# A written-out order of an attention and gated-MLP kernel replaced by another order, with paired tail stores and a last batch stored by half tiles

## The chip, the cores and the metric

The kernel runs on one core of one Trainium2 chip. The metric is the device time of one execution in microseconds (us). The core has five instruction streams that run side by side: TensorE (PE: matmuls, with PEld for its weight loads), VectorE (DVE), ScalarE (ACT), GpSimd (POOL) and SyncE (SP, which only issues transfers). Transfers between memory and the chip run on 16 DMA engines. Each stream executes its instructions strictly in the order in which they were written, so an instruction that waits holds up everything behind it on its engine.

## The reference

Eight batches, twelve heads, 448 positions, head size 64. Queries and keys are normalised by their root mean square, then softmax attention is computed, and the result of all heads (768 columns) goes through a gated MLP with a mixing over positions.

```python
def _attn_ref(q, k, v, g_q, g_k):
    q_n, k_n = (rmsnorm(q, g_q), rmsnorm(k, g_k))
    scores = scale * np.matmul(q_n, k_n.transpose(0, 1, 3, 2))
    attn = np.exp(scores - np.max(scores, axis=-1, keepdims=True))
    attn = attn / (np.sum(attn, axis=-1, keepdims=True) + 1e-09)
    return np.matmul(attn, v)

def _moe_ref(x, w_in, w_spatial, b_spatial, w_out):
    h = np.maximum(x @ w_in, 0.0)
    u, v = h[..., :d_ff // 2], h[..., d_ff // 2:]
    v_n = (v - mean(v)) / np.sqrt(var(v) + 1e-06)
    v_s = np.einsum('ts,bsd->btd', w_spatial, v_n) + b_spatial[None, :, None]
    return (u * v_s) @ w_out
```

The output is 8 x 448 x 768 in float32, 11 MB; the inputs q, k and v are 33 MB.

## The kernel before

The whole order of work is written out in one string, `PLAN`, of some 2,000 words. A loop at the end of the kernel reads it word by word and calls one function for each. A word has the form name.arguments/slots/engine: `S.5.3/01` is `op_S(G=5, u=3)` with the PSUM banks 0 and 1. No scheduler moves anything afterwards; the order of the words is the order of each engine's instructions.

Heads are taken in groups of four, so a batch b has three groups G = 3b, 3b+1 and 3b+2, and there are 24 groups. The stages of a group are these, with the letters of the words:

- `L.G.i` loads q (i = 0), k (1) or v (2) of a group as a 448 KB tile into one of ten `raw` slots (line 281; `l` are half loads of group 0). The loads are issued by SP. A slot is taken again when its last reader is done.
- `Q` squares a tile (ACT, DVE or POOL, line 373 or 375), `R` sums the squares on DVE (line 386), `I` and `J` make the inverse root on ACT (lines 399 and 404), `N` multiplies (POOL or DVE, line 419).
- `P` with `K` turn a tile by TensorE and copy it out (lines 438, 356, 457); for later groups `T` with `Z` turn it by a transposing DMA (line 474) instead.
- `S` makes scores (line 499, eight small matmuls for each word), `E` is their exponential on ACT (line 507). There are 168 of each, seven for each group.
- `F` casts v to bf16. `s`, `a` and `b` are passes over the exponentials (line 534) for the sums of the softmax and the two halves of the output; `D` and `d` invert the sums on ACT (lines 553 and 557), `X` multiplies on DVE (line 563).
- `V`, `W` and `U` are the matmuls with `w_in` (lines 579, 594, 632), `c` and `u` their relu, `B`, `M`, `m` and `A` the normalisation, `H` the mixing over positions (line 647), `G` the gate on DVE (line 654).
- `O.b.m.h` is the product with `w_out` for tile m of batch b and column half h (line 663, four matmuls), `o` copies it to one of five `os` slots (line 354 on ACT, 356 on DVE), and `t.b.m` stores the tile (lines 679 and 681). Positions 384 to 447 of two neighbouring batches share one tile, m = 3: 64 rows of each batch.
- `z.n` are n matmuls on constants in the head (line 247), `w`, `ws`, `wo` and `wb` are the loads of the weights by POOL's queue (lines 310, 325, 328 and 333), `x` copies rows of `w_in` into another order.

A copy into an `os` slot waits until the store that read the slot before has landed. That wait, the slots of `raw` and the eight PSUM banks are the couplings on which the change bears.

Of the kernel before, what the change touches and what calls it, by code (L numbers as in the profile page):

```python
# [27 lines left out]
K.1.1/1/v P.2.0/6 K.2.0/1/v P.1.0/2 K.1.0/2/v s.0.2.0/3 E.0.0/4 S.0.3/45 E.0.3/5 S.0.2/67 E.0.2/6 F.0//g a.0.6.0/0
N.2.1/3 Q.3.0/1/v s.0.6.0 s.0.3.0 a.0.3.0 a.0.2.0 S.1.4/12 E.1.4/7 Q.4.0/0/v F.1//v s.0.0.0 S.1.6/45 E.1.6/8 S.1.0/67
a.0.1.0 E.1.0/9 S.1.5/12 E.1.5/a S.1.2/45 E.1.2/b R.3.0 P.2.1/6 s.0.4.0 S.1.1/12 E.1.1/c b.0.1.0/7 b.0.4.0 L.7.0/3  # L30
a.0.0.0 s.0.5.0 S.1.3/45 E.1.3/d a.0.4.0 R.4.0 K.2.1/2/v wo w.0 a.0.5.0 s.0.1.0 S.2.6/12 b.0.3.0 s.1.0.0/6 E.2.6/e
Q.3.1/2 R.3.1 I.3 J.3 Q.4.1/1 R.4.1 a.1.3.0/4 b.0.5.0 a.1.1.0 s.1.2.0 I.4 S.2.1/12 E.2.1/f Q.5.0/0 a.1.6.0 s.1.1.0
L.2.2/8 L.5.1/5 L.6.1/0 Y.4/5 s.1.6.0 N.3.1/0/v N.3.0/1/v S.2.0/12 s.1.4.0 s.1.3.0 b.0.6.0 s.1.5.0 L.3.2/9 J.4 N.4.0/2
N.4.1/3 D.0/0 b.1.5.0/3 b.1.6.0 E.2.0/g y.4//v L.7.1/6 a.1.2.0 d.0 S.2.3/12 D.1/1 R.5.0 P.3.1/5 P.3.0/6 K.3.1/3/v
K.3.0/3/v E.2.3/h Y.1/1 y.1//v Y.0/2 y.0//v S.3.4/56 d.1 Q.6.0/2/a a.1.0.0 E.3.4/i a.1.4.0 b.1.0.0 S.3.6/12 E.3.6/j
b.0.2.0 S.3.1/56 E.3.1/k X.0.0 P.4.1/0 Q.5.1/1/v K.4.1/0/v b.1.1.0 S.2.2/12 b.1.4.0 b.1.3.0 E.2.2/l R.5.1 L.4.2/7
S.3.3/56 E.3.3/0 b.0.0.0 b.1.2.0 a.1.5.0 w.1 I.5 X.1.1 X.1.0 Y.2/0 X.0.1 y.2//v S.2.5/12 E.2.5/6 P.4.0/3 K.4.0/0/v
S.3.5/56 E.3.5/2 Y.3/4 y.3//v L.8.0/4 S.3.2/12 Q.6.1/0 R.6.1 F.2//g J.5 R.6.0 E.3.2/8 s.2.1.1/70 s.2.6.1 s.2.3.1
s.2.5.1 F.3//g S.3.0/56 a.2.1.1/34 a.2.6.1 S.2.4/12 L.5.2/8 s.2.2.1 a.2.3.1 E.3.0/9 E.2.4/1 a.2.2.1 s.2.0.1 Q.7.1/1
R.7.1 Q.7.0/0/a R.7.0 N.5.0/0 a.2.5.1 a.2.0.1 S.4.4/56 E.4.4/3 s.2.4.1 b.2.2.1/12 N.5.1/1 a.2.4.1 b.2.3.1 b.2.1.1  # L40
D.2/1 b.2.0.1 b.2.4.1 b.2.5.1 Q.8.0/2 P.5.0/5 K.5.0/2/v L.8.1/9 L.9.1/2 P.5.1/6 K.5.1/1/v I.6 D.3/0 J.6 N.6.1/3 x.2
L.9.0/5 d.2 X.2.0 V.0.2.1/7 I.7 T.6.1/0 V.0.1.1/0 N.6.0/2 T.6.0/3 d.3 b.2.6.1 S.4.1/56 V.0.1.0 V.0.2.0 X.2.1 E.4.1/c
V.0.1.2 Q.9.1/1/a X.3.1 S.5.1/56 E.5.1/7 X.3.0 S.4.0/12 E.4.0/d V.0.2.2 c.0.2//v c.0.1//v R.9.1 V.0.0.1/3 J.7 L.10.0/0
U.0.0.1/4 S.4.6/56 E.4.6/4 S.5.3/12 x.0 U.0.2.2/7 L.11.1/1 B.0.2 Q.8.1/0 U.0.0.2 V.0.0.0 F.5//g E.5.3/5 N.7.0/0/v
Z.6/3/v S.5.2/56 S.5.0/01 E.5.0/b R.8.1 N.7.1/1 T.7.1/1 U.0.0.0 U.0.1.1/2 U.0.1.2 R.8.0 u.0.0//v E.5.2/a S.4.5/01
E.4.5/8 U.0.1.0 S.6.4/56 E.6.4/l U.0.2.1 S.4.3/01 I.8 E.4.3/0 V.0.0.2 u.0.1//v c.0.0//v S.4.2/56 F.4//g Q.9.0/1
E.4.2/h J.8 N.8.1/3 U.0.3.0/4 U.0.3.2 S.5.5/01 E.5.5/f S.5.6/23 E.5.6/k B.0.1 R.9.0 U.0.2.0 U.0.3.1 s.4.0.1/56
# [673 lines left out]
```

## Time and profile before

| | us |
|---|---|
| median of three runs | 274.83 (273.71 to 276.78) |
| profiled execution, device time | 274.1 |
| its span, first to last instruction | 272.2 |
| what lies around the span | 1.9 |
| TensorE busy | 256.3 |
| ACT busy | 215.8 |
| DVE busy | 212.2 |
| POOL busy | 120.9 |
| bytes moved | 57.27 MB, mean 210 GB/s |

A busy TensorE is not a TensorE at its peak: a matmul that was issued and waits for its place counts as busy, and small matmuls on different parts of the array overlap. The DMA share in the views of stretches is the mean busy share of the 16 engines and can exceed 1 where packets overlap.

### The profile page before, as it was taken

The page shows a single profiled execution, that of the slowest core. Times are in us where ns is not written, and L with a number is a line of the kernel's source. Part 1 is how long each engine was busy: PE and PEld are TensorE (multiplying, and loading weights), DVE is VectorE, ACT ScalarE, POOL GpSimd, SP SyncE. Part 2 cuts the span into 40 slices and gives each one's busy share as a digit, 9 for nine tenths or more (in the row PEclk, how much of TensorE's full clock was granted, in tenths as well). Part 3 has the DMA queues.
Part 4 walks back from the last instruction along what each step waited for, and adds up shares of the span by engine and source line. Part 5 has one row for each costly group of instructions (what it writes and reads, how often), then busy time and mean ns, then how long its engine had stood idle before and what let it go on. Part 6 is the DMA issues. An engine that isn't in the chain of part 4 may idle for free.

```text
span 272.2 us, 9903 instructions
## 1 busy us (share of the span) xinstructions
PE 256.3 (94%) x4243; PEld 126.7 (47%) x4262; DVE 212.2 (78%) x385; ACT 215.8 (79%) x353; POOL 120.9 (44%) x92
## 2 busy tenths in 40 slices
PE   7898988999999998999999999999999999999992
PEld 3454555335444463454444454443444545455551
DVE  6978997897899978788799968984986555388651
ACT  3879999899999887999899999997889967224041
POOL 2756679879483994468384778011220000000000
PEclk9979999999999999999999999999999999999999
DMA  7999999999999999999999996793275102023255
GB/s 251 315 302 352 259 351 296 210 237 266 213 330 221 261 290 251 258 336 240 301 178 354 183 243 190 211 198 67 118 164 91 60 2 60 2 116 152 83 213 192
DMA packets 59235, 57.27 MB, mean 210 GB/s; under 512 B 35448, under 2 KB 54840, under 8 KB 59192
## 3 DMA queue, kind: packets, MB, share of 16 engines
q1 hardware_dynamic: 57416, 53.42, 75.3%
q0 software_dynamic: 1488, 2.76, 5.4%
q8 instruction: 33, 0.54, 0.8%
q10 hardware_dynamic: 288, 0.46, 0.5%
q14 instruction: 10, 0.08, 0.1%
HBM read 38.56 MB, written 11.01 MB: 182 GB/s over the span
## 4 chain that ended last, share of the span: by engine, by line
PE 69%; DMA 8%; DVE 8%; ACT 5%; issue 3%; POOL 1%; SPq 0%; DVEq 0%
PE ps L534 14%; PE ps L663 12%; PE ps L632 12%; PE ps L499 11%; PE ps L579 9%; PE ps L647 8%; DMA raw<-in_k_dram 6%; ACT et L507 3%; DMA out_dram<-os 2%; PE ps L594 2%; DVE s L607 1%; DVE ss L386 1%; DVE gt L654 1%; DVE xt L563 1%; POOL nrm L419 1%
## 5 line engine op out<-in xcount | busy, mean ns | idle before, releaser
L507 ACT ACTIVATE et<-ps 128x896 bf16<-128x896 f32 x168 | 146.1, 920 | 16.0 <-PE ps L499 14.7
L419 POOL TENSOR_TENSOR nrm<-raw,rs 128x896 bf16<-128x896 f32 x32 | 53.7, 1689 | 33.9 <-DVE nrm L419 10.9
L499 PE MATMUL ps<-qT,kT 64*32 64x448 bf16 x1344 | 60.1, 355 | 3.9 <-ACT et L507 1.8
L375 POOL TENSOR_TENSOR sqt<-raw 128x896 f32<-128x896 f32 (+1 forms) x28 | 46.0, 1652 | 19.4 <-DVE sqt L375 5.8
L534 PE MATMUL ps<-et,vt 64*32 64x448 bf16 x1344 | 48.2, 350 | 1.2 <-issue 0.8
L386 DVE TENSOR_REDUCE ss<-sqt 128x14 f32<-128x896 f32 x46 | 48.4, 1075 | 0.5 <-ACT sqt L373 0.4
L663 PE MATMUL ps<-w_out,gt 128*128 128x384 bf16 x224 | 42.5, 326 | 0.1
L499 PEld LDWEIGHTS <-kT 64*32 64x32 bf16 x1344 | 20.8, 89 | 34.7 <-issue 25.1
L563 DVE TENSOR_TENSOR xt<-ps,rc 128x448 bf16<-128x448 f32 x48 | 27.5, 617 | 11.1 <-PE ps L534 7.4
L663 PEld LDWEIGHTS <-gt 128*128 128x128 bf16 x224 | 21.0, 98 | 18.7 <-issue 4.1
L534 PEld LDWEIGHTS <-vt 64*32 64x32 bf16 x1344 | 22.7, 92 | 14.9 <-issue 5.2
L647 PE MATMUL ps<-w_spT,vs 128*128 128x448 bf16 (+1 forms) x128 | 28.1, 353 | 0.2 <-DVE vs L623 0.2
L534 PE MATMUL ps<-et,ones 64*32 64x448 bf16 x672 | 26.7, 350 | 0.0
L304 POOL CAST vt<-raw 128x896 bf16<-128x896 f32 x16 | 14.8, 931 | 25.6 <-PE ps L534 11.9
L632 PE MATMUL ps<-xt,w_in 128*128 128x448 bf16 x104 | 26.0, 353 | 0.0
L354 ACT ACTIVATE os<-ps 128x384 f32<-128x384 f32 x25 | 12.3, 498 | 17.1 <-PE ps L663 10.6
L607 DVE BATCH_NORM_STATS2 s<-vs 128x6 f32<-128x512 bf16 (+1 forms) x32 | 21.9, 685 | 2.7 <-ACT vs L570 2.2
L356 DVE COPY os<-ps 128x384 f32<-128x384 f32 x31 | 16.9, 549 | 8.5 <-PE ps L663 6.9
L654 DVE TENSOR_TENSOR gt<-ps,us 128x448 bf16<-128x448 f32 (+2 forms) x48 | 20.0, 458 | 3.9 <-PE ps L647 1.6
L632 PE MATMUL ps<-xt,w_in_x 128*128 128x448 bf16 x88 | 22.3, 353 | 0.1
L579 PE MATMUL ps<-w_in,xt 128*128 128x512 bf16 x70 | 20.1, 381 | 0.6 <-issue 0.5
L579 PEld LDWEIGHTS <-xt 128*128 128x128 bf16 x144 | 12.2, 98 | 17.0 <-issue 6.9
(65 smaller groups left out, 277.0 us busy)
## 6 DMA issues: line engine op xcount, KB each, us to landing
raw<-in_v_dram SPq DMA_DIRECT2D x24, 448.0 KB, 5.6
raw<-in_q_dram SPq DMA_DIRECT2D x23, 448.0 KB, 6.8
raw<-in_k_dram SPq DMA_DIRECT2D x23, 448.0 KB, 5.9
out_dram<-os SPq DMA_DIRECT2D x24, 384.0 KB, 3.3
w_in<-in_moe_w_in_dram POOLq DMA_DIRECT2D x3, 512.0 KB, 9.6
w_in_x<-w_in SPq DMA_DIRECT2D x12, 128.0 KB, 4.9
out_dram<-os SPq DMA_DIRECT2D x8, 192.0 KB, 4.4
w_out<-in_moe_w_out_dram POOLq DMA_DIRECT2D x1, 768.0 KB, 12.1
```

The costliest lines, as they stand in the source:

```text
L375: port(eng, eng.tensor_tensor(out=t, in0=x, in1=x, op=ALU.mult))
L386: dve.tensor_reduce(out=sss[G % 3][:, i].rearrange("p r c -> p (r c)"), in_=sqt[where.pop(("sq", G, i))].rearrange("p r (c d) -> p (r c) d ...
L419: port(eng, eng.tensor_tensor(out=nrm[sl[0]].rearrange("p c r d -> p r c d"), in0=raw[where["raw", G, i]].rearrange("p r (c d) -> p r c d" ...
L499: pe.matmul(out=ps[at:at + 32, sl[n], 0:S], lhsT=kT[64 * r:64 * r + 64, c, 64 * hh + 32 * x:64 * hh + 32 * x + 32], rhs=qT[64 * r:64 * r + ...
L507: act.activation(out=ets[sl[0]].rearrange("p n (t c) -> p n t c", c=C), in_=ps[:, a:b + 1:b - a, 0:S].rearrange("p n (c t) -> p n t c", c= ...
L534: pe.matmul(out=ps[to:to + 32, where[kind, G][0], 0:S], lhsT=w, rhs=et_of(G, r, c)[at:at + 64], start=(n == 1), stop=(n == C), tile_positi ...
L563: dve.tensor_tensor(out=xts[b % 2][:, 2 * g + half, :], in0=ps[:, where.pop(("ab"[half], G))[0], 0:S], in1=rcs[where["rc", G]], op=ALU.mult)
L579: pe.matmul(out=ps[:, bank, :], lhsT=xts[b % 2][:, j, 128 * m:128 * m + 128], rhs=w_of(b, j)[:, DH:], start=(n == 1 and j == 2 * g), stop= ...
L607: dve.bn_stats(out=s6, in_=vss[b % SLOTS["vs"]][rows, m, :])
L632: pe.matmul(out=ps[:, bank, 0:S], lhsT=w_of(b, j)[:, 128 * f:128 * f + 128], rhs=xts[b % 2][:, j, :], start=(n == 1 and j == 2 * g), stop= ...
L647: pe.matmul(out=ps[:, sl[0], 0:S], lhsT=vns[b % SLOTS["vs"]][rows, m, 128 * f:128 * f + 128], rhs=w_spT[rows, n, :], start=(m == 0), stop= ...
L663: pe.matmul(out=ps[:, sl[0], 0:384], lhsT=gt[:, f, at:at + 128], rhs=w_out[:, f, 384 * h:384 * h + 384], start=(f == 0), stop=(f == 3))
```

## The change

`PLAN` is replaced by another order of the same work. Four things change beside the order itself.

The filler matmuls of the head: the four later `z` words are gone (9 matmuls), `z.22` stays, and twelve words of a new kind, `h`, stand in the first part, each two matmuls of 64 rows by 32 columns on constants.

The store of a tile that two batches share, `t.b.3`, is one transfer now instead of two of 64 rows each. Its destination is written as a pattern of 2 x 64 x columns.

The stores of batch 7 are by column halves, `t.7.m.h`, each 128 rows of 384 columns; three of them are issued from ACT's queue.

The engine of some steps: squares on ACT 16 where there were 13 (whole tiles), on POOL 22 for 27, on DVE 8 for 6; casts of v on POOL 19 for 16; copies of `os` 28 on ACT and 28 on DVE for 25 and 31.

```diff
 PLAN = """
-l.1.0/0 setup l.0.0/1/a q.1.0/0/v r.1.0 q.0.0/1/v l.1.1 gl.0//s gl.1//s r.0.0 l.0.1//a q.0.1//a r.0.1 q.1.1//g r.1.1
+l.1.0/0 setup l.0.0/1/a l.0.1//a l.1.1 L.1.1/2 gl.0//s gl.1//s q.0.0/0/a q.1.0/1/v r.1.0 q.0.1//a r.0.0 r.0.1 q.1.1//a
...
-O.7.1.0/1 o.7.1.0//a t.7.1 O.7.2.0/4 o.7.2.0/4/a O.7.2.1/7 o.7.2.1//v t.7.2 O.7.3.0/6 o.7.3.0/3/v O.7.3.1/0 o.7.3.1//a
-t.7.3
+t.6.0 O.7.2.0/2 o.7.2.0/1/v t.7.2.0 O.7.2.1/0 o.7.2.1//v t.7.2.1 o.7.1.1//a t.7.1.1//a O.7.3.0/5 o.7.3.0/0/v t.7.3.0
+O.7.3.1/6 o.7.3.1//a t.7.3.1 O.7.0.1/7 o.7.0.1/3/a t.7.0.1 O.7.0.0/3 o.7.0.0//a t.7.0.0//a
 """
...
+    def op_h(sl, e, r):
+
+        at = slice(64 * r, 64 * r + 64)
+        for _ in range(2):
+            pe.matmul(out=ps[0:32, sl[0], 0:S].rearrange("p (c t) -> p c t", c=C), lhsT=ident[at, 0:32],
+                      rhs=ident[at, None, 0:T].to_broadcast([64, C, T]), start=True, stop=True, tile_position=(64 * r, 0))
+
...
-    def op_t(sl, e, b, m):
+    def op_t(sl, e, b, m, *half):
         t = oss[where["os", b, m]]
-        assert where["o", b, m, 0] and where["o", b, m, 1]
+        cols = slice(384 * half[0], 384 * half[0] + 384) if half else slice(0, DM)
+        assert all(where["o", b, m, h] for h in half or (0, 1))
         eng = engines[e or "s"]
         if m == 3:
-            for n in range(2):
-                eng.dma_start(out=out[b - 1 + n, TAIL:S], in_=t[64 * n:64 * n + 64])
-            return
-        eng.dma_start(out=out[b, 128 * m:128 * m + 128], in_=t)
+            eng.dma_start(out=out[b - 1:b + 1, TAIL:S, cols], in_=t[:, cols])
+        else:
+            eng.dma_start(out=out[b, 128 * m:128 * m + 128, cols], in_=t[:, cols])
```

The functions above `op_t` and below `op_z` are seven lines further down in the changed kernel, so that line 663 is 670 there, and so on.

The first place is the end of SP's queue. These are the last stores of before (the slot of `os` has the numbers 136 to 140; L681 is a whole tile, L679 the two halves of a shared tile):

```order
L681 DMA out_dram<-os_139 128x768
L681 DMA out_dram<-os_136 128x768
L681 DMA out_dram<-os_138 128x768
L681 DMA out_dram<-os_137 128x768
L681 DMA out_dram<-os_140 128x768
L679 DMA out_dram<-os_139 64x768 x2
```

And these are the last stores on SP's queue now, from the shared tile of batches 4 and 5 on (slot 137) to the end; L686 is a shared tile, L688 any other:

```order
L686 DMA out_dram<-os_137 2x64x768
L688 DMA out_dram<-os_136 128x768
L688 DMA out_dram<-os_139 128x768
L688 DMA out_dram<-os_140 128x768
L688 DMA out_dram<-os_138 128x768
L688 DMA out_dram<-os_137 128x768
L688 DMA out_dram<-os_136 128x768
L688 DMA out_dram<-os_139 128x768
L688 DMA out_dram<-os_138 128x768
L688 DMA out_dram<-os_137 128x384 x2
L686 DMA out_dram<-os_136 2x64x384 x2
L688 DMA out_dram<-os_139 128x384
```

The two transfers of 64 rows became one whose outermost count is 2. The shared tile of batches 6 and 7 was the last thing stored; now it stands ahead of the halves of tile 0, the second of which is ACT's last instruction (`t.7.0.0//a`) and is not in this list.

The second place is DVE's order near the end, where the slot 137 of that list is filled again. Before, this is the stretch from the first gates of batch 6 to the gates of batch 7 (COPY os is `o`, TENSOR_SCALAR vs is `A`, the gt rows are `G`):

```order
L654 TENSOR_TENSOR gt<-ps,us_133 128x448 x2
L623 TENSOR_SCALAR vs_132<-vs_132,mv_142,rv_146 128x512 x2
L654 TENSOR_TENSOR gt<-ps,us_133 128x448
L356 COPY os_137<-ps 128x384
L572 TENSOR_SCALAR us_134<-ps 128x448 x2
L356 COPY os_139<-ps 128x384
L654 TENSOR_TENSOR gt<-ps,us_134 128x384
```

Now:

```order
L630 TENSOR_SCALAR vs_132<-vs_132,mv_142,rv_146 128x512 x2
L661 TENSOR_TENSOR gt<-ps,us_133 128x448 x2
L630 TENSOR_SCALAR vs_132<-vs_132,mv_142,rv_146 64x512
L363 COPY os_137<-ps 128x384
L630 TENSOR_SCALAR vs_132<-vs_132,mv_142,rv_146 128x512
L661 TENSOR_TENSOR gt<-ps,us_133 128x448 x2
L661 TENSOR_TENSOR gt<-ps,us_134 128x384
```

The copy into slot 137 (`o.5.0.1/1/v`) stands now ahead of the last normalisation of batch 7 (`A.7.1`), which every `H.7` needs; before, the normalisations of batch 7 were all done when DVE came to a copy into slot 137.

The third place is ACT's order in the first part, around the 16th exponential (et rows are `E`, sqt are squares, rc the inverse sums, ls and rs the roots). Before:

```order
L507 ACTIVATE et15_106<-ps_63 128x896
L404 ACTIVATE rs1_122<-ls1_119 128x28
L553 ACTIVATE rc0_113<-ps_63 128x448
L507 ACTIVATE et16_107<-ps_63 128x896
L557 ACTIVATE rc0_113<-rc0_113 128x448
L553 ACTIVATE rc1_114<-ps_63 128x448
L507 ACTIVATE et17_108<-ps_63 128x896
L557 ACTIVATE rc1_114<-rc1_114 128x448
L373 ACTIVATE sqt2_76<-raw1_65 128x896
```

Now, at the same exponentials:

```order
L514 ACTIVATE et14_105<-ps_63 128x896
L380 ACTIVATE sqt0_74<-raw4_68 128x896
L514 ACTIVATE et15_106<-ps_63 128x896
L560 ACTIVATE rc1_114<-ps_63 128x448
L514 ACTIVATE et16_107<-ps_63 128x896
L514 ACTIVATE et17_108<-ps_63 128x896
L564 ACTIVATE rc1_114<-rc1_114 128x448
L406 ACTIVATE ls1_119<-ss1_116,eps_154 128x28
```

ACT squares a k tile of group 5 (slot 4 of `raw`, `Q.5.1/0/a`) between the 15th and the 16th exponential; before, DVE squared that tile (`Q.5.1/1/v`). Up to the 28th exponential ACT squares three tiles more than before, and its copy of `kT` ahead of the first exponential is gone.

More of the change, by code (lines that the diff above doesn't have):

```diff
@@ L28 @@
[L28 to L47, printed above, removed]
@@ L138 @@
[L138 to L141 removed]
+l.1.0/0 setup l.0.0/1/a l.0.1//a l.1.1 L.1.1/2 gl.0//s gl.1//s q.0.0/0/a q.1.0/1/v r.1.0 q.0.1//a r.0.0 r.0.1 q.1.1//a
+r.1.1 i.0 j.0 n.0.0//g i.1 j.1 n.0.1//g gA z.22/7 gB/0 h.0/1 gC n.1.1//g Q.1.1/2/a R.1.1 h.1/2 h.1/3 L.1.0/3 Q.1.0/0/a
@@ new lines @@
+L.10.1/5 b.4.6.1 S.7.3/01 E.7.3/e d.5 a.4.3.1 Q.10.0/0 b.4.2.1 a.4.1.1 X.4.0 L.11.1/8 b.4.4.1 L.7.2/9 b.4.1.1 b.4.3.1
+X.4.1 L.11.0/1 T.8.1/1 T.8.0/1 S.7.5/67 X.5.1 X.5.0 E.7.5/0 S.6.6/01 E.6.6/g V.1.0.0/2 V.1.0.1 S.7.2/67 E.7.2/h
+N.9.0/1 S.7.6/45 E.7.6/l W.0/3 c.0.3//v c.1.3//a L.12.1/4 S.7.4/01 T.9.0/0 E.7.4/3 S.6.4/67 E.6.4/i V.1.1.2/4
+U.1.1.0/5 V.1.1.0 R.10.0 B.0.3 V.1.1.1 V.1.2.1/3 V.1.0.2 B.1.3 V.1.2.0 S.7.1/01 M.0 m.0 A.0.2 A.0.0 A.0.3 A.0.1
+c.1.1//a c.1.0//a B.1.0 S.7.0/67 E.7.0/2 B.1.1 U.1.1.1 V.1.2.2 c.1.2//a B.1.2 E.7.1/a H.0.1/4 F.7//g G.0.1 H.0.2/2
@@ new lines @@
+G.0.2 Q.10.1/2 R.10.1 S.6.1/67 Q.11.1/1/a S.6.2/01 E.6.1/1 U.1.2.2/3 E.6.2/7 U.1.2.0 U.1.2.1 M.1 u.1.2//a Q.11.0/0/a
+I.10 H.0.3/4 G.0.3 H.0.0/2 Z.8/1/v G.0.0 S.6.0/67 E.6.0/c S.6.5/01 S.8.0/34 U.1.1.2 R.11.1 Z.9/0/v O.0.2.0/2
+o.0.2.0/0/v J.10 E.6.5/d L.6.2/7 N.10.1/2 L.12.0/2 L.8.2/3 L.14.0/0 U.1.3.2/6 u.1.1//v R.11.0 U.1.0.2/7 N.10.0/0/v
+U.1.0.1 U.1.3.1 L.9.2/9 S.9.6/01 E.8.0/4 Q.12.1/2/a I.11 J.11 m.1 A.1.0 S.9.1/23 E.9.1/j O.0.2.1/5 R.12.1 O.0.0.1/4
+o.0.0.1/1/a o.0.2.1//a U.1.0.0 u.1.0//v U.1.3.0 L.13.1/5 L.15.1/6 E.9.6/6 O.0.0.0/2 o.0.0.0//a F.6//g O.0.1.1/3
@@ new lines @@
+S.9.5/45 E.9.5/f L.13.0/7 t.0.0 s.6.6.1/70 T.10.1/1 u.1.3//a A.1.1 s.6.4.1 A.1.3 A.1.2 Q.12.0/1/v s.6.0.1 s.6.2.1
+s.6.5.1 s.6.3.1 s.6.1.1 D.7/0 N.11.1/3 L.15.0/8 Q.14.0/0 S.8.5/12 E.8.5/9 S.8.2/45 D.6/1 Q.13.1/2 E.8.2/b N.11.0/1
+H.1.1/6 G.1.1 H.1.0/0 a.6.1.1/12 a.6.4.1 G.1.0 R.12.0 S.8.4/67 E.8.4/8 a.6.5.1 S.9.3/45 o.0.1.1/2/a E.9.3/k d.6
+H.1.3/0 H.1.2/6 G.1.3 T.10.0/3 d.7 I.12 J.12 F.8//g O.0.1.0/7 G.1.2 a.6.3.1 o.0.1.0//v S.8.1/34 b.6.3.1/05 E.8.1/5
+a.6.0.1 S.8.3/67 a.6.6.1 b.6.1.1 R.13.1 a.6.2.1 X.6.0 X.7.0 b.6.0.1 b.6.4.1 b.6.2.1 b.6.5.1 b.6.6.1 X.6.1 F.9//g
@@ new lines @@
+S.17.3/67 E.17.3/2 R.21.1 S.16.1/45 E.16.1/b O.3.3.1/2 U.4.1.0/1 U.4.1.2 S.17.4/67 Q.20.1/0 u.4.3//a E.17.4/c
+o.3.3.1//v t.3.3 R.20.0 F.17//v R.20.1 S.16.2/45 E.16.2/l V.4.1.0/2 V.4.1.2 Q.23.1/1/a U.4.1.1 u.4.1//v I.20 V.4.1.1
+S.17.2/67 R.23.1 E.17.2/6 Q.22.1/2/v S.16.4/45 V.4.0.1/0 V.4.2.2 U.4.2.0/1 V.4.0.2 U.4.2.1 c.4.1//v B.4.1 J.20
+N.20.1/0 E.16.4/9 T.20.1/1 S.17.5/67 E.17.5/7 S.18.5/45 E.18.5/k V.4.0.0 U.4.2.2 u.4.2//v V.4.2.1 c.4.2//a O.2.1.0/2
+c.4.0//v S.17.6/67 E.17.6/0 o.2.1.0//v L.22.2/2 s.16.3.1/45 s.16.0.1 Q.21.0/0 s.16.4.1 S.18.4/01 E.18.4/e s.16.5.1
@@ new lines @@
+X.18.1 F.20//g X.18.0 O.3.1.0/3 o.3.1.0//a H.4.3/7 G.4.3 X.19.0 E.21.6/8 m.5 A.5.1 U.5.3.2/4 U.5.3.0 S.21.4/56
+E.21.4/k S.20.3/01 E.20.3/4 O.4.2.0/3 U.5.3.1 o.4.2.0/4/v t.3.2 u.5.3//v A.5.0 S.20.4/56 E.20.4/d s.20.5.1/72 A.5.3
+s.20.6.1 s.20.0.1 S.22.4/01 E.22.4/a a.20.5.1/34 s.20.1.1 s.20.3.1 t.0.1 s.20.4.1 S.22.5/56 E.22.5/i s.20.2.1 D.20/0
+d.20 Z.23/3/v A.5.2 H.5.2/0 H.5.3/1 G.5.2 a.20.2.1 G.5.3 S.23.0/56 D.21/1 b.20.3.1/70 b.20.5.1 E.23.0/2 b.20.1.1
+a.20.3.1 b.20.6.1 b.20.2.1 S.22.1/12 d.21 E.22.1/e b.20.0.1 a.20.0.1 b.20.4.1 X.21.1 S.22.2/56 a.20.4.1 a.20.6.1
```

186 lines of the change are left out of this document (90 added, 96 removed).

## The prediction

> **What bounds the kernel now.** I read the page first: who is busy, and whose work the chain that ended last is made of.
>
> ```profile
> PE 256.3 (94%) x4243; PEld 126.7 (47%) x4262; DVE 212.2 (78%) x385; ACT 215.8 (79%) x353; POOL 120.9 (44%) x92
> PE 69%; DMA 8%; DVE 8%; ACT 5%; issue 3%; POOL 1%; SPq 0%; DVEq 0%
> ```
>
> TensorE carries 69% of the chain, but ACT and DVE are not far from it. So I read the stretches of ten microseconds, which show who is full where.
>
> ```profile
> core 0: us, PE busy (x) PEld busy (x) DVE busy (x) ACT busy (x) POOL busy (x), PEclk, DMA share, GB/s
> 0.00:10.00 10.00, 8.28 (x41) 3.99 (x41) 7.24 (x20) 4.70 (x9) 3.90 (x10) 1.00 0.84 276
> 10.00:20.00 10.00, 8.49 (x102) 4.70 (x105) 8.14 (x11) 8.03 (x12) 6.40 (x8) 0.83 1.10 298
> 20.00:30.00 10.00, 8.62 (x196) 4.37 (x183) 8.04 (x10) 9.53 (x14) 7.03 (x6) 1.00 1.09 329
> 30.00:40.00 10.00, 8.54 (x189) 5.64 (x188) 9.33 (x15) 9.69 (x16) 6.54 (x6) 1.00 1.08 323
> ...
> 110.00:120.00 10.00, 9.79 (x115) 4.13 (x107) 8.03 (x13) 9.50 (x15) 3.98 (x5) 1.00 1.15 317
> ...
> 250.00:260.00 10.00, 10.00 (x58) 5.40 (x57) 7.58 (x17) 1.63 (x5) 0.00 (x0) 1.00 0.30 120
> 260.00:270.00 10.00, 7.22 (x44) 4.10 (x42) 3.74 (x10) 3.38 (x8) 0.00 (x0) 1.00 0.69 262
> ```
>
> The reader sees three regimes. Up to 40 us ACT is full (9.53, 9.69) and TensorE is not; the DMA engines are full as well (shares of 1.08 to 1.10). In the middle TensorE, ACT and the DMA engines are all near their limit (9.79, 9.50, 1.15). At the end TensorE alone is full (10.00), and after its last matmul only a copy and stores are left. A reorder of the same work moves the time only where one of these limits is not kept: the head, the waits of the middle, and the end.
>
> **The end.** These rows are from the chain, the time line and the transfers of the last 18 us (the transfers with the median from issue to landing; for L679 the issue time as min/median/max in ns).
>
> ```profile
> 260.72 6.51 PE ps L663 x40
> 267.25 0.49 ACT os L354
> 267.77 1.11 SPq L679 DMA_DIRECT2D out_dram<-os  x2
> L681 SPq DMA_DIRECT2D out_dram<-os x7: 332/332/383, 255.0 to 266.6; - x7
> L679 SPq DMA_DIRECT2D out_dram<-os x2: 477/530/583, 267.8 to 268.3; - x2
> out_dram<-os SPq DMA_DIRECT2D x7, 384.0 KB, 2.3
> out_dram<-os SPq DMA_DIRECT2D x2, 192.0 KB, 2.6
> GB/s 0 89 430 355 0 0 0 0 0 0 0 0 0 0 314 410 423 416 184 198 416 417 430 287 232 403 239 177 423 273 48 218 184 389 34 0 0 0 0 0
> ```
>
> The last matmul ends at 267.25, which I call E. The last store is issued at 268.3 and lands 2.6 later, at 270.9; the span ends at 272.2, 1.3 after that and 4.95 after E. Four matmuls of a word `O` take 6.51 x 4/40 = 0.65.
>
> Now the last five words `O` are 7.2.1, 7.3.0, 7.3.1, 7.0.1 and 7.0.0, and the stores are halves. The very last one, on ACT's queue, is 196,608 B. A 384 KB store lands 2.3 after its issue: 0.33 of issue, 393,216 B at 430 GB/s = 0.91, and 1.06 for the rest. The half needs 0.33 + 0.46 + 1.06 = 1.85; issued at E + 0.51 it lands at E + 2.36, and the span would end at E + 3.66, 1.3 earlier than now. I keep 1.1, since 192 KB rows took 2.6.
>
> But the shared tile is stored in a new way, and that is the term I weigh most. Every large transfer of before has an outermost count of 128, 64 or 32 rows, which 16 engines can share evenly. The new store runs over 2 x 64 rows; its outermost count is 2. No row shows a transfer of that kind. The lower bound of its price is the row of the whole tile: 2.3 for 384 KB. The upper bound is that only two engines take part: one engine moves 430/16 = 26.9 GB/s, a whole tile is 196,608 B for each of the two, 7.3 us, and the store lands 0.53 + 1.06 + 7.3 = 8.9 after its issue. I take the upper bound: when a transfer is cut into shares by its outer loop, there are only two shares to give.
>
> The Trainium skill, "DMA: Bandwidth & Descriptors", section "Why a DMA increments its semaphore by 16 and not by 1", speaks against the change here: the number of engines is the largest up to 16 that divides the outermost count (other than 1) of both sides, which would be 2. By that rule the sum is the one with 8.9 below, by the row of 2.3 it is that of the first rival; no run here shows yet which holds.
>
> With two engines the end goes so: `O.7.3.0` ends at E - 1.95, its copy on DVE takes 0.55 and the wake-up 0.06, so the store is issued at E - 1.34. The second half comes right behind it on the same two engines, together 7.3 us of data: landing at E - 1.34 + 0.53 + 1.06 + 7.3 = E + 7.55, and the end of the span at E + 8.85 instead of E + 4.95. That is **+3.9**.
>
> **The wait for a slot.** The shared tile of batches 4 and 5 sits in slot 137 of `os`, and `o.5.0.1` on DVE fills that slot next. Prices of the matmuls come from the chain, of DVE's work from the groups.
>
> ```profile
> 259.20 1.51 PE ps L647 x8
> 251.78 1.14 PE ps L632 x6
> L356 DVE COPY os<-ps 128x384 f32<-128x384 f32 x31 | 16.9, 549 | 8.5 <-PE ps L663 6.9
> L354 ACT ACTIVATE os<-ps 128x384 f32<-128x384 f32 x25 | 12.3, 498 | 17.1 <-PE ps L663 10.6
> L623 DVE TENSOR_SCALAR vs<-vs,mv,rv 128x512 bf16<-128x512 bf16 (+1 forms) x32 | 11.9, 406 | 1.7 <-ACT rv L616 1.5
> ```
>
> From the end of `O.5.3.1` TensorE has six words `U` (12 x 0.19 = 2.3), three `O` (1.95) and three `H` (12 x 0.19 = 2.3) to the end of `H.6.3`, 6.5 us. DVE comes to `o.5.0.1` at about 7: `O.5.0.1` is ready at 5.75, and normalisations and two gates stand ahead. The store is issued at 0.55, after its copy, and lands at 0.55 + 8.9 = 9.45. DVE waits 2.5; behind it stands `A.7.1`, behind that `H.7.3` on TensorE, which has only `H.6.2` (0.76) as cover and would use that up anyhow (7 + 0.55 + 0.41 is already 7.96 against 7.24). So **+2.5**, between 0 (store at 2.3) and 3.5.
>
> **The middle.** Before, one such wait stands in the chain (the last row is from the waits of DVE: us in total, times, longest):
>
> ```profile
> 172.96 6.60 DMA out_dram<-os
> ...
> 179.68 0.56 DVE os L356
> DVE os L356 <- DMA out_dram<-os: 1.3, 1, 1.3
> ```
>
> A store took 6.60 beside loads, and DVE's copy waited 1.3 for it. In the new order the loads stand further ahead of their readers and the slots are reused later, so I credit **-1.0** for that and similar waits (0 to -3). The shared tiles of batches 0 to 3 are stored here too; with two engines each adds 7.3 - 0.9 us to two full engines, while the next copy into their slots stands nine words `E` or more later, 7 us or more on ACT alone: **+0.5** (0 to +3).
>
> **The head.** ACT is its limit up to the 28th exponential.
>
> ```profile
> 12.47 1.00 ACT L455 ACTIVATE kT<-ps,g_col 64x896 bf16<-64x896 bf16 x1
> 13.65 0.32 ACT L399 ACTIVATE ls<-ss,eps 128x28 f32<-128x28 f32 x1 [0.18 <-DVE ss L386]
> 14.00 0.23 ACT L404 ACTIVATE rs<-ls 128x28 f32<-128x28 f32 x1
> 14.53 2.54 ACT L507 ACTIVATE et<-ps 128x896 bf16<-128x896 f32 x3 [0.30 <-PE ps L499]
> ...
> 41.27 2.52 ACT L507 ACTIVATE et<-ps 128x896 bf16<-128x896 f32 x3
> ACT et L507 <- PE ps L499: 2.4, 5, 1.3
> L373 ACT ACTIVATE sqt<-raw 128x896 f32<-128x896 f32 (+1 forms) x14 | 13.0, 926 | 4.1 <-DMA raw<-in_q_dram 3.3 <-DMA raw<-in_k_dram 0.8
> ```
>
> The 28 exponentials run from 14.53 to 43.79 (first and last row shown). Now `kT` is copied by DVE, and one pair of roots moves behind the first exponential: it can start 1.00 + 0.55 earlier. Up to the 28th ACT gains three squares (3 x 0.93) and that pair (0.55), 3.3 in all; of its 2.4 of waiting for scores in the first 45 us about half should go, as all of group 0 is ready at once. Net -1.55 + 3.3 - 1.2 = **+0.6**, between -0.6 and +1.8. The fillers cost nothing: TensorE is idle for 1.72 + 1.51 + 1.38 + 1.46 = 6.1 us in the first 40, more than 24 small matmuls of 0.19 take (4.6); without that idle time they would cost 4.6 less 1.7 for the nine that go. Whether they lift the clock of 0.83 I put at nothing, within half a microsecond.
>
> **The sum.** 274.1 of the profiled execution + 0.6 - 1.0 + 0.5 + 2.5 + 3.9 = **280.6**, which is 2.1% over the median of 274.83; the profiled execution lies 0.3% below that median. The terms' own bounds make this case 276.5 to 284.
>
> **The rivals.** *First, the stores are shared by all 16 engines* and land in 2.3. Then the slot costs nothing and the end is 1.1 shorter: 274.1 + 0.6 - 1.0 - 1.1 = 272.6 (269 to 276), not slower than before. It decides if a shared tile of 384 KB lands in under about 4 us. For it speaks that every store in the rows is fast; against it, that none has two as its outer count. Chance 0.25.
>
> *Second, stores on two engines, but the order gains in the middle* what they cost: -4 there in place of -1.0, and most of the 2.5 hidden, gives 276. For it: the copies into `os` alone wait 6.9 and 10.6 us for TensorE (rows L356 and L354), which another order may use. Against: TensorE is at 9.79 there. Chance 0.08.
>
> *Third, ACT waits for a load in the head.* Before, this chain stands there:
>
> ```profile
> 20.77 15.25 DMA raw<-in_k_dram
> ...
> 36.14 1.09 DVE sqt L375
> ```
>
> A k load issued at 20.77, beside the weights, took 15.25, and DVE's square waited. Now that square is on ACT behind the 15th exponential, at about 13.0 + 14 x 0.84 + 1.85 of two squares + 1.1 of two pairs of roots + 1 of an inverted sum (an estimate: two passes like the copies of 0.50) = 29. Its load stands in the queue about where it stood, so I take 20 again. With 15.25 it lands at 35: up to 6 us in which the exponentials behind it stand. With 4 of it and the forecast's other terms: 284.6. Chance 0.07.
>
> **How the numbers follow.** The forecast's case has 0.60, the first rival 0.25, the second 0.08, the third 0.07. One per cent is 2.75 us, about what a measurement of this kernel tells from no change: faster is under 272.1, slower over 277.6. Of the first rival 0.10 lies under 272.1, 0.13 within and 0.02 above; of the forecast 0.55 lies above and 0.05 within; the second is within; the third is slower. So faster 0.10, same 0.26, slower 0.64. The predicted time is 280.6. The range from 271.5 to 284 leaves out some 0.07 below and 0.08 above; the forecast's own is 276.5 to 284.
>
> **What would show it.** Right: the transfers of the shared tiles (line 686) land in 7 us or more at the end, bytes per second in the last 8 us are near 54 GB/s instead of 400, the span ends some 8 us after the last matmul, and DVE's copy waits for a store in the last 25 us. Wrong: those stores land in 2 to 4 us and the span ends under 4 us after the last matmul. In the head, the 28th exponential ends between 43 and 46; far later, with ACT waiting for a k load, is the third rival.

## The result and the profile after

The changed kernel takes 289.33 us (288.51 to 289.65), the kernel before beside it 275.2. The ratio is 1.051, with a 95% interval of 1.044 to 1.057: slower, and by 8.7 us more than the 280.6 predicted, outside the range. The profiled execution has a span of 287.9. All times are medians of a kernel's undisturbed executions; with a disturbed one of 368.8 us among them, the kernel of the experiments with only the last pair undone would stand at 283.4, the figure that a later expectation uses, in place of 282.4.

The exponentials say when the difference arises. Up to the 28th the changed kernel is ahead by 2.6 us (41.15 against 43.79). At the 112th it is ahead by 2.0 still, at the 140th 3.0 behind (196.0 against 193.0), at the last one 0.8 ahead (228.05 against 228.83). Its last matmul, E, ends at 275.7 against 267.25, and the span goes on for 12.2 us in place of 4.95. So nearly all that shows in the end is lost in the last 60 us, and two things are lost there: one before E, one after it. What the middle lost is hidden behind what the new order and its fillers gained, as the experiments will show.

The busy times on the page, for comparison with the first line of the prediction:

```profile
PE 258.2 (90%) x4277; PEld 126.6 (44%) x4277; DVE 212.5 (74%) x381; ACT 217.4 (76%) x359; POOL 115.4 (40%) x90
```

No engine has more work worth the name; the shares fall because the span grows. Now the end, in the chain and SP's time line of the changed kernel (start, duration; SP's rows are the issue alone):

```profile
248.81 10.92 DMA out_dram<-os
259.82 0.56 DVE os L363
...
260.86 1.30 PE ps L654 x3
262.16 1.28 PE ps L670 x4
263.44 2.40 PE ps L654 x8
265.84 1.95 PE ps L670 x12
267.79 0.76 PE ps L654 x4
268.54 7.16 PE ps L670 x44
```

```profile
274.42 1.15 SPq L686 DMA_DIRECT2D out_dram<-os  x2
275.67 3.15 SPq L688 DMA_DIRECT2D out_dram<-os  x1
```

The shared tile of batches 4 and 5 is stored at 248.81 and takes 10.92; DVE's copy into its slot waits for it, and TensorE waits for DVE. The two halves of the last shared tile are issued at 274.42. The issue of the plain store behind them takes 3.15 us, where that of the three plain stores ahead of them takes 0.33 or 0.34 each. What the DMA engines do then, and what TensorE's clock did in the wait, stands in the stretches of two microseconds (busy PE, PEld, DVE, ACT, POOL, then clock, DMA share, GB/s):

```profile
258.00:260.00 2.00, 0.00 (x0) 0.00 (x0) 0.18 (x1) 0.00 (x0) 0.00 (x0) 0.57 0.13 52
260.00:262.00 2.00, 1.14 (x4) 0.47 (x5) 1.86 (x4) 0.00 (x0) 0.00 (x0) 0.50 0.12 49
262.00:264.00 2.00, 2.00 (x8) 0.85 (x7) 0.45 (x1) 0.49 (x1) 0.00 (x0) 0.50 0.00 2
...
280.00:282.00 2.00, 0.00 (x0) 0.00 (x0) 0.00 (x0) 0.00 (x0) 0.00 (x0) 0.50 0.28 81
282.00:284.00 2.00, 0.00 (x0) 0.00 (x0) 0.00 (x0) 0.00 (x0) 0.00 (x0) 0.50 0.13 51
284.00:286.00 2.00, 0.00 (x0) 0.00 (x0) 0.00 (x0) 0.00 (x0) 0.00 (x0) 0.50 0.12 46
```

In 258 to 260 and in 282 to 286 the share is 0.12 to 0.13, which is 2/16, at 46 to 52 GB/s: two engines, as forecast. The same flow goes on from 260 to 262, when the paired store has landed; by then it is the rest of the plain stores issued behind it at 249.5 to 252.1, the only other transfers under way, which have shares on these two engines as well. And a further row needs notice: after the stall the clock is at 0.50 until about 265. That was in no term of the prediction.

The slot near 250 us is not the only one that copies wait for. These are the waits of copies for stores in the whole run, DVE's and ACT's:

```profile
DVE os L363 <- DMA out_dram<-os: 9.7, 3, 5.0
ACT os L361 <- DMA out_dram<-os: 1.9, 1, 1.9
```

Beside the 5.0 there are 2.3 (DVE) and 1.9 (ACT) at 117.6 us, for the first paired store, issued 13.3 earlier, and 2.4 (DVE) at 180.4, for the second, issued 11.5 earlier. TensorE waits 1.1 and 1.8 behind them.

### The profile page after: what moved, and what is told of

Its sections match the earlier page's. It is cut to its first block, busy times and chain, and to the rows that moved or that the text cites. A ratio compares the mean times of both kernels' runs of the same rounds, so it can differ in the third digit from the quotient of the medians.

```text
span 287.9 us, 9932 instructions
## 1 busy us (share of the span) xinstructions
PE 258.2 (90%) x4277; PEld 126.6 (44%) x4277; DVE 212.5 (74%) x381; ACT 217.4 (76%) x359; POOL 115.4 (40%) x90
## 5 line engine op out<-in xcount | busy, mean ns | idle before, releaser
L506 PE MATMUL ps<-qT,kT 64*32 64x448 bf16 x1344 | 59.2, 353 | 5.5 <-DVE os L363 1.8
L541 PE MATMUL ps<-et,vt 64*32 64x448 bf16 x1344 | 49.5, 350 | 2.0 <-POOL vt L311 1.7
L382 POOL TENSOR_TENSOR sqt<-raw 128x896 f32<-128x896 f32 x22 | 36.8, 1680 | 29.4 <-DVE nrm L426 13.7
L506 PEld LDWEIGHTS <-kT 64*32 64x32 bf16 x1344 | 21.6, 90 | 34.1 <-issue 24.2
L654 PE MATMUL ps<-w_spT,vs 128*128 128x448 bf16 (+1 forms) x128 | 29.1, 366 | 5.2 <-DVE vs L630 5.2
L361 ACT ACTIVATE os<-ps 128x384 f32<-128x384 f32 x28 | 13.4, 493 | 25.4 <-PE ps L670 22.9
L541 PEld LDWEIGHTS <-vt 64*32 64x32 bf16 x1344 | 21.4, 92 | 16.3 <-issue 3.3
L363 DVE COPY os<-ps 128x384 f32<-128x384 f32 x28 | 15.4, 552 | 16.4 <-DMA out_dram<-os 9.7
L311 POOL CAST vt<-raw 128x896 bf16<-128x896 f32 x19 | 17.5, 930 | 13.0 <-DMA raw<-in_v_dram 9.3
L586 PE MATMUL ps<-w_in,xt 128*128 128x512 bf16 x78 | 21.7, 381 | 0.9 <-issue 0.9
```

Of the source, the lines that this page charges most:

```text
L382: port(eng, eng.tensor_tensor(out=t, in0=x, in1=x, op=ALU.mult))
L506: pe.matmul(out=ps[at:at + 32, sl[n], 0:S], lhsT=kT[64 * r:64 * r + 64, c, 64 * hh + 32 * x:64 * hh + 32 * x + 32], rhs=qT[64 * r:64 * r + ...
L541: pe.matmul(out=ps[to:to + 32, where[kind, G][0], 0:S], lhsT=w, rhs=et_of(G, r, c)[at:at + 64], start=(n == 1), stop=(n == C), tile_positi ...
L586: pe.matmul(out=ps[:, bank, :], lhsT=xts[b % 2][:, j, 128 * m:128 * m + 128], rhs=w_of(b, j)[:, DH:], start=(n == 1 and j == 2 * g), stop= ...
L654: pe.matmul(out=ps[:, sl[0], 0:S], lhsT=vns[b % SLOTS["vs"]][rows, m, 128 * f:128 * f + 128], rhs=w_spT[rows, n, :], start=(m == 0), stop= ...
```

## The experiments

Theory: the paired store costs nearly all, in three places (the middle, the slot, the end), since two engines carry it; the new order as such is a gain. The rivals: the order itself loses the middle (B), or the order is most of the loss and the paired store little (C).

### All pairs undone, and each alone

```diff
-            eng.dma_start(out=out[b - 1:b + 1, TAIL:S, cols], in_=t[:, cols])
+            for n in range(2):
+                eng.dma_start(out=out[b - 1 + n, TAIL:S, cols], in_=t[64 * n:64 * n + 64, cols])
```

> The changed kernel with every shared tile stored again as two transfers of 64 rows (in the halves of batch 7 too); order, fillers and half tiles stay. Theory (the paired store on two DMA engines costs the end, the slot wait near 250 us and what the middle loses from 104 us on): the last matmul ends near 267.25 - 2.6 = 264.7, what follows it falls from 12.2 to about 3.7, so 264.7 + 3.7 + 1.9 = 270.3 us (268 to 272.5). Rival B (the new order itself loses the 5 to 6 us of the middle, the paired store only the end and the slot wait): 276 us (274 to 279). Rival C (the paired store is slow to read but hides, the order costs most): 284 us or more.

Measured: **269.5 us** (268.54 to 271.62), ratio to before 0.980 (0.974 to 0.986). Rivals B and C fall. With two transfers in place of one, and nothing else touched, the changed kernel is 20 us faster, and faster than the kernel before. E is at 262.8. The expected 270.3 came near by two misses that offset each other: E came 1.9 earlier than expected, and what follows it was 5.0 long and not 3.7.

The same edit for the last shared tile only (`if b < 7` keeps the pair), and for the three earlier ones only (`if b == 7` keeps it):

> The changed kernel with only the last shared tile (batches 6 and 7, both halves) stored as two transfers of 64 rows; the three earlier ones stay paired. Theory and rival B alike: the span ends 3.7 us behind the last matmul in place of 12.2, the wait for the slot near 250 us stays (about 5 us at TensorE): 289.3 - 8.5 = 280.8 us (279 to 283). Rival C: 286 us or more. Together with the first run of this set it gives the price of the three earlier paired stores: by the theory 280.8 - 270.3 = 10.5 us, by rival B 280.8 - 276 = 4.8 us.

> The changed kernel with the three earlier shared tiles (batches 0 to 5) stored as two transfers of 64 rows; only the last one, in halves, stays paired. Theory: no wait for the slot near 250 us, the middle as in the first run of this set, the end as in the changed kernel: 270.3 + 8.5 = 278.8 us (277 to 281). Rival B: 276 + 8.5 = 284.5 us. Rival C: 286 us or more.

Measured: 282.4 us (281.8 to 284.4) with only the last undone, and 276.1 us (275.5 to 277.4) with only the last kept. So the last pair costs 276.1 - 269.5 = 6.6, the three earlier ones 282.4 - 269.5 = 12.9; together 19.5, against 19.8 between the changed kernel and 269.5. The prices add up. The first of the two expectations lay 1.6 under what came and has it in its range; the second lay 2.7 above and has not: 8.5 for the last pair was too much, since the split kernel's end was not 3.7 long, but 5.0.

And the slot by itself: only the shared tile of batches 4 and 5 is paired.

```diff
+            if b == 5:
+                eng.dma_start(out=out[b - 1:b + 1, TAIL:S, cols], in_=t[:, cols])
+            else:
                 for n in range(2):
```

> The kernel of the first experiment (269.5) with only the shared tile of batches 4 and 5 stored as one transfer of 2 x 64 rows: the wait for the slot alone. By the trace of the changed kernel (DVE's copy waits 5.0 for that store; behind it seven matmuls of line 654 and the four of line 670 run at half the clock and take some 2.1 longer than in the first experiment): 269.5 + 7.1 = 276.6 us (275.5 to 278). By the prediction's own term (+2.5): 272.0 us. If the stall at DVE were absorbed behind TensorE: 269.5.

Measured: **276.1 us** (275.7 to 276.9), so +6.6. The same places in the chain of this kernel, and then in the one with no pair:

```profile
242.87 11.02 DMA out_dram<-os
253.98 0.56 DVE os L363
255.03 1.30 PE ps L654 x3
256.33 1.28 PE ps L670 x4
257.61 2.67 PE ps L654 x8
```

```profile
248.97 0.56 DVE os L363
250.02 0.74 PE ps L654 x3
250.76 0.65 PE ps L670 x4
251.41 1.51 PE ps L654 x8
```

DVE's wait is 5.1 here (5.0 in the changed kernel), and the 15 matmuls behind it take 1.30 + 1.28 + 2.67 = 5.25 us instead of 2.90. The clock went down in the stall and needs 4 to 5 us of matmuls to come back. So a stall of 5 us at TensorE costs 7. In the changed kernel the last matmul before the stall ends at 255.7, the clock falls at about 258.3, and it is up again at about 265.1, 4.2 after the first matmul; in the kernel with the one pair the fall comes 3.2 after the last matmul and the return 4.8 after the first. In both the clock is at half for 6.8 us. The Trainium skill, "TensorE: Matmul & The Clock Gate", section "Part 1: The HAM clock gate", has the drop after an idle window of about 3.4 us and the return after as much sustained work. The traces agree in kind and not in the times: the drop comes earlier (2.6 and 3.2), the return later (4.2 and 4.8), and it is the measured times that a sum should use.

### The pair put into the kernel before

```diff
-            for n in range(2):
-                eng.dma_start(out=out[b - 1 + n, TAIL:S], in_=t[64 * n:64 * n + 64])
+            eng.dma_start(out=out[b - 1:b + 1, TAIL:S], in_=t)
             return
```

> The kernel before with one part of the change alone: a shared tile is stored as one transfer of 2 x 64 rows. Theory: each such store lands 9 to 11 us after its issue; the last one, issued right behind the last copy, puts the end of the span at some 12.7 us behind the last matmul in place of 4.95 (+7.8), and the three earlier ones cost another 2 to 7 in the middle: 285 to 290 us. Rival B (in the middle they hide): 281 to 284 us. Rival C (the paired store costs little by itself): under 279 us.

Measured: **295.6 us** (293.9 to 296.8), +19.7 on the 275.9 of the kernel before beside it, more than the theory's 285 to 290. The end is near the expected 12.7: the last matmul ends at 281.9, the span at 293.6, 11.7 later. The middle is worse than expected. SP's time line and the chain of this kernel at the first paired store:

```profile
102.84 0.62 SPq L678 DMA_DIRECT2D out_dram<-os  x1
...
104.15 7.60 SPq L474 DMA_TRANSPOSE kr<-nrm  x1
```

```profile
104.15 13.97 DMA kr<-nrm
...
188.65 12.09 DMA raw<-in_v_dram
200.86 0.94 POOL vt L304
```

SP needs 7.6 us to issue the transposing transfer behind the store (1.38 in the kernel before, at the same place), and it lands 14 us after its start. All loads behind it in SP's queue are late too. At the second paired store a load of v, issued 0.7 ahead of it, takes 12.09 us. In 108 to 116 us this kernel moves 77 GB/s and the kernel before 274 (the first row is of this kernel, the second of the kernel before):

```profile
108.00:116.00 8.00, 6.68 (x72) 2.39 (x71) 4.28 (x6) 7.19 (x11) 1.69 (x1) 1.00 1.18 77
```

```profile
108.00:116.00 8.00, 7.79 (x99) 3.18 (x87) 5.46 (x9) 7.66 (x12) 3.90 (x3) 1.00 1.19 274
```

The share of 1.18 is no sign that all engines move data in those 8 us: in 108 to 110 us alone it reads 4.06 at 107 GB/s, since packets that overlap are counted several times. Behind that stand these two stretches of this kernel:

```profile
110.00:112.00 2.00, 1.96 (x24) 0.78 (x23) 1.63 (x3) 2.00 (x3) 1.44 (x1) 1.00 0.13 52
112.00:114.00 2.00, 2.00 (x18) 0.71 (x15) 1.12 (x2) 2.00 (x5) 0.00 (x0) 1.00 0.13 48
```

For these four microseconds only two engines' worth of data flows (0.13, 48 to 52 GB/s), while the transposing transfer has yet to land. So two engines that are full hold up other transfers, in an order whose loads are just in time. The next two runs price this in the new order and ask whether it is SP's queue or the two engines.

### Two pairs in the middle, on SP's queue and on ACT's

The kernel with all pairs undone, with the first two shared tiles paired again (`if b < 5`); in the second run their words are `t.1.3//a` and `t.3.3//a`.

> The kernel of the first experiment (269.5) with the shared tiles of batches 0 and 1 and of batches 2 and 3 stored as one transfer of 2 x 64 rows again, on SP's queue; the later two stay split. It prices the loss in the middle without the wait for the slot near 250 us: the three earlier pairs together cost 13.9 (283.4 less 269.5), the slot wait at TensorE and the colder clock behind it were some 6 to 7 of this, so 276 to 278 us. If the two cost nothing by themselves: 269 to 270.

> The same two paired stores, issued from ACT's queue in place of SP's. Theory 1 (the middle loses because SP's issue of the transposing transfers behind the paired store is held some 8 us): most of the loss goes, 270 to 273 us. Theory 2 (it loses because two of the 16 engines are full, and every load and transposing transfer has a share on them): as on SP's queue, 276 to 278 us. Theory 3 (ACT is held in its turn, and its exponentials with it): 278 us or more, with ACT idle behind line 686.

Measured: 275.1 us on SP's queue (+5.6; a little under the expected 276 to 278), **279.9 us** on ACT's (+10.4). Of the first, a part is again a copy: DVE's copy waits 1.6 for the second paired store at 178.3, and TensorE 1.1 behind it.

Where the second loses 4.8 more can be read. At the 112th exponential the two kernels are 0.4 apart, at the 140th 5.4. Between lies this wait of TensorE in the kernel with ACT's queue, which the other does not have:

```profile
PE ps L506 <- DMA qT<-nrm: 4.6, 1, 4.6
```

It ends at 181.4. The transfer that it waits for is the first row below (SP's time line in this kernel; ACT issues the second paired store at 165.0). The second fence has the same transfer with the stores on SP's queue:

```profile
167.71 1.38 SPq L481 DMA_TRANSPOSE qT<-nrm  x1
171.63 4.63 SPq L481 DMA_TRANSPOSE kr<-nrm  x1
...
177.50 3.77 SPq L481 DMA_TRANSPOSE qT<-nrm  x1
```

```profile
165.84 1.52 SPq L481 DMA_TRANSPOSE qT<-nrm  x1
167.46 0.58 SPq L687 DMA_DIRECT2D out_dram<-os  x1
```

On SP's queue the transposing transfer goes out 1.6 ahead of the paired store and lands after 4.4. On ACT's queue the store goes out 2.4 earlier and so ahead of that transfer, which is issued in an ordinary 1.38 and lands after 13.7. TensorE stalls, and its clock is at half from 179.3 to 186.1. So theory 1 falls: this transfer lost its time after its issue and behind a store in another queue. The issues of the next two rows are longer as well (4.63 and 3.77, where the same two take 1.89 and 1.25 with no pair). ACT is not held by the store's issue (0.5 and 1.1 us), so theory 3 had the number and not the cause. Theory 2 has the cause that fits the rows, with too low a number: the two engines are what the transfers share.

### What makes it two engines

The destination's loops change places, and nothing else:

```diff
-            eng.dma_start(out=out[b - 1:b + 1, TAIL:S, cols], in_=t[:, cols])
+            eng.dma_start(out=out[b - 1:b + 1, TAIL:S, cols].rearrange("n t c -> t n c"), in_=t[:, cols])
```

> The changed kernel with each shared tile still in one transfer, but its destination walked rows first: the pattern is 64 x 2 x columns in place of 2 x 64 x columns, the source stays 128 rows. (The rows of the two batches come out interleaved, so the 64 tail rows of the two batches are not where the reference has them; bytes, counts of transfers and order are the same.) Theory (the outermost count, 2 or 64, sets how many engines move it): each shared tile lands in 2.3 to 3 us when nothing else runs, as any other tile, and the whole kernel runs as the one with two transfers of 64 rows did (269.5) or up to 1.3 us below it, since fewer transfers are issued at the end: 268 to 270 us. Rival (a transfer over two far regions of memory is slow as such, whichever loop is outside): 286 to 292 us, as the changed kernel.

Measured: **268.4 us** (268.2 to 270.9). The same bytes to the same two regions in one transfer: with 64 as the outermost count no copy waits for a store of a shared tile, and where the landing is seen it is 2.2 to 6.0 us (median 3.3) after the issue:

```profile
DMA to landing us min/median/max: 2.2/3.3/6.0
```

It is the outermost count alone.

The same question for tiles of one batch, in the kernel before (the cut of one of the three tiles is shown):

```diff
+        if (b, m) == (5, 0):
+            eng.dma_start(out=out[b, 128 * m:128 * m + 122], in_=t[0:122])
+            eng.dma_start(out=out[b, 128 * m + 122:128 * m + 128], in_=t[122:128])
+            return
```

> The kernel before with three of its whole-tile stores cut by rows: tile 1 of batch 3 into 124 + 4 rows, tile 0 of batch 4 into 120 + 8, tile 0 of batch 5 into 122 + 6. Theory (the number of engines divides the outermost count: 4 engines for 124, 15 for 120, 2 for 122; each moves 21 to 27 GB/s): the 124 rows land 5.1 to 6 us after their issue, the 120 rows 2.3 to 2.6, the 122 rows 8.6 to 10.3. Rival (rows are dealt out evenly, and only a pattern whose outer count is below 16 is slow): all three land in 2.3 to 2.6.

Measured: 274.4 us in its one execution; it was made for its rows and not for its time. The landing of the first and the third is not recorded; the flow shows them. The stretches behind the stores of 124 rows (issued at 211.8), of 120 rows (241.5, with the next whole tile right behind) and of 122 rows (255.3):

```profile
215.50:217.50 2.00, 2.00 (x89) 1.08 (x74) 0.71 (x2) 1.48 (x3) 0.00 (x0) 1.00 0.23 75
...
244.00:245.00 1.00, 1.00 (x8) 0.55 (x6) 1.00 (x3) 0.38 (x2) 0.00 (x0) 1.00 0.98 393
...
258.00:260.00 2.00, 2.00 (x14) 1.12 (x13) 1.70 (x5) 0.40 (x2) 0.00 (x0) 1.00 0.14 46
```

Shares of 0.23 and 0.14 are four engines and two, as the rule of division has it; the rival of an even deal falls. The 120 rows are fast (3.0 to landing), but 0.98 does not tell 15 engines from 16. The 124 rows took some 7 us, from 212.5 to 219.5, where 5.1 to 6 to landing was expected: in the first four microseconds the flow was 28 and 44 GB/s, far below four engines' rate. The rule of the Trainium skill that the prediction cited ("DMA: Bandwidth & Descriptors", section "Why a DMA increments its semaphore by 16 and not by 1") has the number of engines as the largest up to 16 that divides the outermost counts. The runs agree with it for all four counts that they can tell apart: 2, 64, 122 and 124.

This run also shows, at a place without loads or transposing transfers, what a store on two engines does to others. Behind the 122 rows three whole tiles land 4.99, 4.49 and 4.51 after their issue; in the kernel before the stores at the same places take 2.81, 2.29 and 2.31.

### The fillers and the half tiles

Both runs start from the kernel with all pairs undone (269.5). Without the twelve `h` words:

> The kernel of the first experiment without the twelve h words (24 matmuls of 64 x 32 on constants); everything else stays. Theory 1 (the fillers keep the granted clock at 1.00 from 14 to 20 us, and this gives the head its 2.6 us): without them the clock there falls to 0.5 to 0.65 and the 28th exponential ends at 42.5 to 43.8 in place of 41.0; 271 to 272 us. Theory 2 (the order of the head gives them, the fillers nothing): the 28th exponential ends at 41.0 within 0.4, 269.5 us. Theory 3 (the fillers cost their own time): earlier than 40.6, 268.5 us or less.

Measured: 270.5 us (270.0 to 270.8). The 28th exponential ends 3.0 later. The stretches with the fillers, then without them:

```profile
14.00:16.00 2.00, 1.86 (x35) 1.04 (x22) 1.30 (x3) 2.00 (x4) 1.53 (x2) 1.00 1.07 383
16.00:18.00 2.00, 1.89 (x31) 0.86 (x29) 1.37 (x3) 2.00 (x6) 0.97 (x2) 1.00 1.06 380
```

```profile
14.00:16.00 2.00, 2.00 (x32) 0.73 (x23) 1.37 (x2) 1.86 (x4) 1.67 (x3) 0.50 1.07 384
16.00:18.00 2.00, 2.00 (x21) 0.91 (x18) 0.68 (x1) 1.92 (x4) 0.93 (x2) 0.50 1.09 385
```

The 28th exponential without them, in ACT's time line:

```profile
42.29 1.72 ACT L514 ACTIVATE et<-ps 128x896 bf16<-128x896 f32 x2
```

With the fillers the clock is 1.00, without them 0.50 from 11.2 us to 21.4, at nearly the same flow of transfers. The row of two exponentials, the 27th and the 28th, ends at 44.01, against 41.04 with the fillers and 43.79 in the kernel before. So theory 1 holds for the head, and the new head without fillers is no earlier than the old one. What its order gives by itself is not separated: the kernel before has the `z` words, and its clock is at 0.50 for 3.4 us only, 16.1 to 19.5. In the time, about 1.0 of the 3.0 is left, and that lies within the spread of the runs at 269.5 (268.5 to 271.6); the expected 271 to 272 was too high.

The last batch by whole tiles again, each where its second half stood (one of the four tiles is shown):

```diff
-o.7.2.0/1/v t.7.2.0 O.7.2.1/0 o.7.2.1//v t.7.2.1
+o.7.2.0/1/v O.7.2.1/0 o.7.2.1//v t.7.2
```

> The kernel of the first experiment (all shared tiles as two transfers of 64 rows) with the last batch stored by whole tiles again, each where its second half stood, on the same queue. Its end was 5.0 us behind the last matmul with half tiles. Prediction's claim (half tiles shorten the end by 1.1): 270.6 us. Rival (with half tiles SP has 9 transfers to issue in the last 10 us, the last of which goes out 1.2 behind the last matmul; whole, the last store goes out 0.5 behind it and lands 2.3 later, so the end is 0.5 + 2.3 + 1.3 = 4.1): 268.6 us. Neither: 269.5.

Measured: 268.96 us (268.75 to 269.21), ratio to before 0.977 (0.972 to 0.982). It ends 4.9 behind the last matmul, where 5.0 stood with half tiles and the rival expected 4.1; its time is between the rival's 268.6 and 269.5, and not to be told from 269.5. The half tiles bring nothing. This kernel, and the one with half tiles, are faster than both kernels of the case.

## Why the prediction was wrong, step by step

The direction, the two engines, and the path at the slot and at the end were right. The step that failed is the price of the paired stores: at 8.9 us each, with nobody held up but a copy into the same slot, they were put at 0.5 + 2.5 + 3.9 = 6.9. Measured they cost 5.6 + 6.6 + 6.6 = 18.8. The sum was 274.1 + 0.6 - 1.0 + 0.5 + 2.5 + 3.9. It missed by 8.7 and not by 12 because another miss went the other way: without the pairs the change gains 5.7 (275.2 to 269.5), where 0.4 was forecast. That the two offset each other in part was luck.

- **Two engines for the paired store: right**, with the run that only turns the loops round as the proof. The first rival (shared by 16 engines) is wrong.
- **The price of one such store, 8.9 us to landing: too low**, and the terms below rest on it. It went by 430/16 = 26.9 GB/s for each engine, a rate of all sixteen with nothing beside it. Measured: 10.92 and 11.02 to landing at the slot, or 196,608 B in some 9.3 us, 21 GB/s for each engine, and 13.3 and 11.5 until a copy could go on in the middle; in quiet stretches an engine moved 23 to 26.
- **The shared tiles of batches 0 to 3, +0.5: the term that failed worst.** Measured +5.6. The prediction looked only for a copy that waits for the slot, and gave it 7 us or more in hand. Copies did wait (1.9 to 2.4 in the changed kernel), since the stores took 11.5 and 13.3 there. Beside them the loads and the transposing transfers waited, which have shares on the same two engines; the run on ACT's queue shows what one such transfer can cost. "Two full engines" stood in the text, and no reader of those engines was looked for. How the 5.6 divides between the two kinds of wait is not settled.
- **The slot 137, +2.5: 6.6 to 7.1.** The path was right (DVE's copy, the normalisation behind it, then `H`). DVE came to the copy 6.0 after the issue, near the forecast's 6.45; the landing of 10.92 in place of 9.45 - 0.55 = 8.9, with DVE 0.5 earlier, turns the wait of 2.5 into 5.0. The other 2.1 are the lower clock behind the stall, which had no term.
- **The end, +3.9: +7.25 in the trace, +6.6 by the runs.** The issue came at E - 1.3, as forecast. But the 7.3 us of data took some 10.6 (last landing at E + 10.9, not E + 7.55). In the first two microseconds only 30 GB/s flowed, and the other stores of the last batch have shares on the same two engines; no run separates these two. The half tiles, worth 1.1 by the first rival, were worth nothing.
- **The head, +0.6: -2.6 at the 28th exponential.** Without the fillers its +0.6 comes out near (44.01 - 43.79 = +0.2), but at a clock that is at half for 10.2 us where the kernel before has 3.4, so this is no proof of its reading of ACT's queue. What failed is "Whether they lift the clock of 0.83 I put at nothing": they lift it from 0.50 to 1.00 for ten microseconds. The third rival (ACT waits for the k load of group 5) did not come.
- **The order in the middle, -1.0 (0 to -3): about -3.3 in the trace, -1.8% in the time (0.978 to 0.986).** That is the run without fillers and pairs (270.5) against the kernel before. ACT's waits for scores in the whole run fall, first before, then there:

```profile
ACT et L507 <- PE ps L499: 14.7, 29, 1.5
```

```profile
ACT et L514 <- PE ps L506: 8.7, 16, 1.0
```

That the gain comes from these waits is not shown by a run of its own. The prediction read this wait for the first 45 us only. Its second rival, an order that gains 4 in the middle, was right in this part, but it took the stores' costs from the same low prices.

By the runs, the sum closes: 269.5 without pairs, + 5.6 + 6.6 + 6.6 for the middle, the slot and the end = 288.3, against 289.3 measured.

## What to carry to other kernels

When two transfers are made one, look at the outermost count of both sides first: a 2 there took away fourteen engines, whatever the inner counts were. And a transfer that fills a few engines is to be priced by everything that is in flight beside it, not only by who waits for it. When a stall of TensorE is long (5 us here), add the half clock behind it to the sum; and a few tiny matmuls in a head where TensorE has pauses can move the head by 3 us, though little of it may reach the end.
